# Two FFN batches at a time by seven block products, and gate products on ScalarE, in a fused attention and mixture-of-depths kernel

## The chip, the cores and the metric

One Trainium2 core. Its engines run instruction queues of their own: PE (TensorE, matrix products; PEld is its weight loads), ACT (ScalarE), DVE (VectorE), POOL (GpSimd), and SP, which issues most DMAs. The time is the device time of one execution in microseconds (us). A second number, the span, comes from a profiled execution: from the first to the last instruction that the hardware profiler recorded.

## The reference

For 8 batches of 8 heads, 1152 tokens and head dimension 64, all float32, queries are averaged in pairs, so there are 576 rows per batch. Attention is followed by a mixture of depths: the 128 rows of each batch with the best gate score pass through a two-layer FFN and are added back, weighted.

```
q_pool = q.reshape(B, H, S // 2, 2, D).mean(axis=3)
attn   = softmax(q_pool @ k.T / sqrt(D)) @ v         # (B, H, 576, 64)
x      = attn rearranged to (B, 576, 512)
scores = x @ w_gate
for b in range(B):
    top = the 128 rows with the largest scores[b]
    xe  = x[b, top]
    h   = maximum(xe @ w1, 0)                        # w1: 512 x 1024
    ye  = h @ w2                                     # w2: 1024 x 512
    out[b, top] = xe + sigmoid(scores[b, top]) * ye  # other rows: out = x
```

## The kernel before

The class `_Plain` writes out each engine's order by hand; no scheduler moves anything. A pair is two heads of a batch, and a half is 288 of a pair's 576 query rows: 8 batches x 4 pairs x 2 = 64 halves, numbered h = 0 to 63; s is h mod 2. The loop in `run` issues for half h, in this order:

- at s=1, on SP's queue: `load_pair` (keys `kb`, queries `qb`) and `load_values` (`v_sb`) of the pair two further on, and `stored`, the output rows of an earlier pair;
- `scores(h)`: nine PSUM tiles of products of keys and queries on PE (L818), each turned into `p` by an exp on ACT (L825);
- ACT copies of row sums: `side_by_side` at s=0 (L887, `groups`), `spread` at s=1 (L902, `sums`, which reads `total`, a DVE reduction at L893);
- `units(mid=True)`: pieces of the FFN work of an earlier batch that are marked "mid". These come between the scores and the values product on PE;
- `gated` (DVE: L979 and L981), `folded` (POOL adds tiles of `p` to `acc`, L857; DVE reduces, L862 and L872), and `multiplied`, on POOL (L925): `prod` = `avb` times the gate weights;
- at s=0, `prepare_pair` for the next pair (POOL L732, DVE transposes L735 and L739);
- `weighted(h-1)`: the values product on PE (L836) and its copy `two` on ACT (L844), which frees the PSUM tile; then POOL adds its two parts into `av` (L846) and DVE transposes that into `avb` (L915);
- `added` (L893) at s=0, `normalized` at s=1 (DVE `rec` L954, POOL `x` L956), and `units(mid=False)`, the other pieces.

An engine takes its instructions in the order in which they were issued: a piece put at "mid" stands behind the exps of half h and ahead of `two` of half h-1.

All PE results share one pool of four PSUM tiles of two banks each (`banks`). The FFN of a batch is a generator, `routed(b)`, created when the batch's gate scores are complete (half 8b+10). Its pieces for batches 0 to 5: `groups` of the score line on ACT in half 8b+11; DMA of the line through DRAM; the rank of each row by comparison on DVE (L1083, L1092, L1102) in halves 8b+13 to 8b+15; picks (L1166), `index` (L1175) and the gathering indirect DMA of 128 rows into `xe` (L1183, POOL's queue) in 8b+16; transposes on PE (L1197) in 8b+18; layer 1 (L1208, with relu on ACT, L1216) at mid of 8b+19; layer 2 (L1221) at mid of 8b+20; then scaling on ACT (L1240), addition on POOL (L1245) and a scattering indirect DMA. Batch 5's layer 2 and most of batches 6 and 7 come after the last half, in `run`'s last lines (`older`, `old` and `new` are batches 5, 6 and 7). L1044 is a DVE product, `diag`, of batch 7 only.

Of the kernel before, what the change touches and what calls it, by code (L numbers as in the profile page):

```python
# [10 lines left out]
P = 128  # L11
BLK = 32
# [522 lines left out]
class _Plain:  # L535
# [10 lines left out]
    def __init__(self, ctx, tc, q, k, v, moe_w_gate, moe_w1, moe_w2, capacity, out):  # L546
# [27 lines left out]
        assert 0 < self.TAIL < P and self.Dm == self.ND * P and self.Dm <= 512  # L574
        assert self.F == self.NFC * P and self.NFC % 4 == 0
# [15 lines left out]
        self.w_gate = self.const.tile([P, self.NPAIR, BLK], F32, name="w_gate")  # L591
        self.w1 = self.const.tile([P, self.ND, self.F], F32, name="w1")
        self.w2 = self.const.tile([P, self.NFC, self.Dm], F32, name="w2")

# [21 lines left out]
    def constants(self):  # L616
# [13 lines left out]
        slot_i = self.ffn.tile([P, self.Sp], I32, name="cmp", bufs=1)  # L630
        nc.gpsimd.iota(slot_i[:, :], pattern=[[1, self.Sp]], base=0, channel_multiplier=0)
        self.slot_f = const.tile([P, self.Sp], F32, name="slot_f")
        nc.vector.tensor_copy(self.slot_f[:, :], slot_i[:, :])
# [34 lines left out]
    def line_of_scores(self):  # L668

        line = self.ffn.tile([P, self.NT * P], F32, name="sc_row")  # L670
        self.nc.gpsimd.memset(line[0:1, self.Sp :], 0.0)
        return line
# [11 lines left out]
    def load_gate(self):  # L684
        gate = self.w_gate_in.rearrange("(n j d) -> n j d", n=self.NPAIR, j=2)
        for j, ds, rows in self.quarters():
            self.nc.sync.dma_start(self.w_gate[rows, :, :], _rows_of(gate[:, j, ds], BLK))
# [9 lines left out]

    def load_pair(self, b, hp):  # L700

        nc = self.nc
        kb = self.load.tile([P, self.KB, BLK], F32, name="kb")
        qb = self.load.tile([P, self.QB, 2, BLK], F32, name="qb")
        for j, ds, rows in self.quarters():
            of = self.k[b, 2 * hp + j, :, ds]
            nc.sync.dma_start(kb[rows, :, :], of.rearrange("(i n) d -> i n d", i=BLK))
        for j, ds, rows in self.quarters():
            of = self.q[b, 2 * hp + j, :, ds].rearrange("(i m) d -> i m d", i=BLK)
            nc.sync.dma_start(qb[rows, :, :, :].rearrange("i n r d -> i (n r) d"), of)  # L710
        return {"k": kb, "q": qb, "b": b, "hp": hp}

    def load_values(self, pair):


        nc, hp = self.nc, pair["hp"]
        v_sb = pair["v"] = self.load.tile([P, 2, self.NC, self.D], F32, name="v_sb", bufs=3)
        of = self.v[pair["b"], 2 * hp : 2 * hp + 2]
        of = of.rearrange("j (i g c) d -> g i j c d", i=BLK, c=self.NC)
        for g in range(P // BLK):  # L720
            nc.sync.dma_start(
                v_sb[g * BLK : (g + 1) * BLK, :, :, :].rearrange("i j c d -> i j (c d)"),
                of[g].rearrange("i j c d -> i j (c d)"),
            )
# [16 lines left out]
    def load_first(self, b, hp):  # L741
# [3 lines left out]
        kb = self.load.tile([P, self.KB, BLK], F32, name="kb")  # L745
        kn = kb.rearrange("p n d -> p (n d)").rearrange("p (c j d) -> p c j d", c=NC, j=2)
        acc = self.work.tile([P, G, 2 * self.HALF], F32, name="acc")
        third = self.QB // 3
        qn = acc.rearrange("p u n -> p (u n)")[0 : 3 * BLK, 0 : 4 * third * D]
        qn = qn.rearrange("p (j m d) -> p j m d", j=2, d=D)  # L750
        v_sb = self.load.tile([P, 2, NC, D], F32, name="v_sb", bufs=3)
# [11 lines left out]
        return {"k": kn, "q": qn, "v": v_sb, "b": b, "hp": hp}  # L763

    def prepare_first(self, pair):
# [5 lines left out]
        acc = self.work.tile([P, G, 2 * self.HALF], F32, name="acc")  # L771
        qp = acc.rearrange("p u n -> p (u n)")[0:rows, 0 : 2 * third * D]
        qp = qp.rearrange("p (n j d) -> p n j d", j=2, d=D)
# [76 lines left out]
    def folded(self, half):  # L850
# [9 lines left out]
        fold = self.small.tile([P, 2, G * nb], F32, name="fold")  # L860
# [21 lines left out]
    def side_by_side(self, of):  # L882

        n = of.shape[-1]
        to = self.small.tile([BLK, P // BLK, n], F32, name="groups")
# [33 lines left out]
    def multiplied(self, half):  # L919

        pair, hb, hp = half["pair"], self.HB, half["pair"]["hp"]
        if half["s"] == 0:
            pair["prod"] = self.work.tile([P, self.QB, BLK], F32, name="prod")
        ns = slice(half["s"] * hb, (half["s"] + 1) * hb)
        self.nc.gpsimd.tensor_tensor(  # L925
            out=pair["prod"][:, ns, :],
            in0=pair["avb"][:, ns, :],
            in1=self.w_gate[:, hp : hp + 1, :].broadcast_to([P, hb, BLK]),
            op=ALU.mult,
        )  # L930
# [42 lines left out]
    def gated(self, half):  # L973
# [5 lines left out]
        nc.vector.tensor_reduce(pair["red"][:, ns], pair["prod"][:, ns, :], AX.X, ALU.add)  # L979
# [17 lines left out]
    def routed(self, b, part):  # L997
# [13 lines left out]
        if b < self.B - 1:  # L1011
# [17 lines left out]
            sc_row = ffn.tile([P, NT * P], F32, name="sc_row")  # L1029
# [11 lines left out]
        else:  # L1041

            diag = ffn.tile([P, self.QB, BLK], F32, name="diag", bufs=1)
# [34 lines left out]
        for t, rows in tiles:  # L1078
            at = t * P
            cmp = ffn.tile([P, Sp], F32, name="cmp", bufs=1)  # L1080
# [20 lines left out]
            tie = ffn.tile([P, P], F32, name="tie", bufs=1)  # L1101
# [35 lines left out]
        for s0, w in self.slots:  # L1137
            pick = ffn.tile([P, NT, P], F32, name="pick", bufs=1)
            index = ffn.tile([P, 1], I32, name="index")
            own_gate = ffn.tile([P, 1], F32, name="own_gate")  # L1140
            if b == self.B - 1:
# [3 lines left out]
                    in0=self.slot_f[:, s0 : s0 + w].unsqueeze(1).broadcast_to([P, NT, w]),  # L1145
# [36 lines left out]
            xe = ffn.tile([P, self.Dm], F32, name="xe")  # L1182
# [18 lines left out]
            yield mid  # L1201

            hT = ffn.tile([P, self.NFC, P], F32, name="hT")
            for f0 in range(0, self.NFC, 4):
                pv = self.banks()[:, 0, :].rearrange("p (c n) -> p c n", n=P)
                for f in range(4):
                    for c in range(self.ND):
                        nc.tensor.matmul(  # L1208
                            pv[:, f, 0:w],
                            lhsT=self.w1[:, c, (f0 + f) * P : (f0 + f + 1) * P],  # L1210
                            rhs=xeT[:, c, 0:w],
                            start=(c == 0),
                            stop=(c == self.ND - 1),
                        )
                    if f == 3:
                        nc.scalar.activation(hT[:, f0 : f0 + 4, 0:w], pv[:, :, 0:w], AF.Relu)  # L1216
                    yield "hidden" if f0 + f == self.NFC - 1 else False

            ps = self.banks()[:, 0, :]
            for f in range(self.NFC):  # L1220
                nc.tensor.matmul(  # L1221
                    ps[0:w, 0 : self.Dm],
                    lhsT=hT[:, f, 0:w],
                    rhs=self.w2[:, f, :],
                    start=(f == 0),
                    stop=(f == self.NFC - 1),
                )
                yield False
            if b == self.B - 1:
                nc.vector.scalar_tensor_tensor(  # L1230
                    out=xe[0:w, :],
                    in0=ps[0:w, 0 : self.Dm],
                    scalar=own_gate[0:w, 0:1],
                    in1=xe[0:w, :],
                    op0=ALU.mult,
                    op1=ALU.add,
                )
            else:
                y = ffn.tile([P, self.Dm], F32, name="y", bufs=1)
                nc.scalar.activation(  # L1240
                    y[0:w, :], ps[0:w, 0 : self.Dm], AF.Copy, scale=own_gate[0:w, 0:1]
                )
                if b < self.B - 2:
                    yield True
                nc.gpsimd.tensor_tensor(out=xe[0:w, :], in0=y[0:w, :], in1=xe[0:w, :], op=ALU.add)  # L1245
            nc.gpsimd.indirect_dma_start(
                out=rows_out,
                out_offset=bass.IndirectOffsetOnAxis(ap=index[0:w, 0:1], axis=0),
                in_=xe[0:w, :],
                in_offset=None,  # L1250
                bounds_check=(b + 1) * Sp - 1,
                oob_is_err=False,
            )
            yield True

    def counted(self):
# [3 lines left out]
        flags = self.ffn.tile([P, n], F32, name="cmp", bufs=1)  # L1260
# [46 lines left out]
    def run(self):  # L1307
# [10 lines left out]
        if loaded:  # L1318
            self.load_values(loaded)
        self.load_gate()  # L1320
        weights = self.weight_loads()
        for h in range(n_halves + 1):
            if h < n_halves:
# [6 lines left out]
                else:  # L1330
                    loaded = None
                    if n + 2 < len(pairs):
                        loaded = self.load_pair(*pairs[n + 2])
                        self.load_values(loaded)
                    if n > 1:
                        self.stored(halves[h - 4]["pair"])
                if h > 1:
                    next(weights, None)
                half = {"pair": pair, "s": s}
                halves.append(half)  # L1340
                self.scores(half)
                if h > 1:

                    of = halves[h - 2 - s]["pair"]
# [8 lines left out]
                if h > 1:  # L1353
                    self.multiplied(halves[h - 2])
# [42 lines left out]
        pieces(older, self.NFC - 2)  # L1397
        pieces(new, 1)
        pieces(older, 2)
        pieces(new, 3)  # L1400
        pieces(older)
        pieces(old, self.NFC)
        pieces(new, 1)
        low = self.counted()
        pieces(old, self.NFC - 3)
# [66 lines left out]
```

## The time and the profile before

| | |
|---|---|
| runs | 708.6, 706.26, 708.48 us; median 708.48 |
| profiled execution | 706.64 us; span 704.8 us; granted PE clock 0.998 |
| busy, share of the span | PE 99%, PEld 73%, DVE 70%, ACT 63%, POOL 69% |
| DMA | 82.86 MB, mean 118 GB/s |
| largest groups, busy us | L825 320.2 (ACT), L818 295.2 and L836 294.6 (PE), L857 266.3 (POOL), L862 251.3 (DVE) |
| FFN on PE, busy us | L1208 59.3, L1221 57.3 |

Busy time counts an instruction from its start to its end, so a DVE or POOL instruction that waits inside its span counts as busy. A line such as L1208 is a line of the kernel before. In a group's line the columns are: line, engine, operation, output and inputs with their shapes, count; busy us, mean ns of one; idle time of the engine ahead of them and what ended it.

### The profile page before, as it was taken

To read this page: it belongs to the slowest core of one execution; us is meant where nothing else is said; L and a number is where in the kernel's file an instruction comes from. 1 tells how busy PE (TensorE), PEld (TensorE's weight loads), DVE (VectorE), ACT (ScalarE), POOL (GpSimd) and SP (SyncE) were. 2 spreads that over 40 slices of the span, in tenths; PEclk is the share of its full clock that TensorE was granted. 3 is DMA by queue.
4 is the path that set the end of the run, shared out by engine and by line. 5 is a ranking of instruction groups with operands and counts; after the bars stand their busy time and mean duration, and the time that the engine had idled before them with its cause. 6 is when DMAs were issued, how large, how long until landed. Compare 5 with 4: busy or idle time off the path is not lost.

```text
span 704.8 us, 23397 instructions
## 1 busy us (share of the span) xinstructions
PE 694.4 (99%) x9948; PEld 516.8 (73%) x9948; DVE 496.5 (70%) x793; ACT 444.5 (63%) x963; POOL 485.1 (69%) x452
## 2 busy tenths in 40 slices
PE   8999999999999999999999999999999999999996
PEld 5668899996758866688656887578775787766573
DVE  3877777996559965498754988559774697689540
ACT  6677778777547775477746776467754777477210
POOL 5877777868658695586955779467874877686520
PEclk9999999999999999999999999999999999999999
DMA  8888887858486483756928468382775728432200
GB/s 175 172 178 180 171 166 137 146 116 161 85 149 111 85 162 75 145 97 111 172 40 159 81 129 160 66 148 61 161 130 85 135 56 169 83 72 62 45 31 35
DMA packets 389490, 82.86 MB, mean 118 GB/s; under 512 B 376640, under 2 KB 376640, under 8 KB 389376
## 3 DMA queue, kind: packets, MB, share of 16 engines
q1 hardware_dynamic: 387872, 76.49, 58.1%
q0 software_dynamic: 1280, 4.20, 1.8%
q8 instruction: 80, 1.31, 0.8%
q10 hardware_dynamic: 224, 0.59, 0.3%
q14 instruction: 34, 0.28, 0.1%
HBM read 69.65 MB, written 11.59 MB: 115 GB/s over the span
## 4 chain that ended last, share of the span: by engine, by line
PE 89%; POOL 5%; issue 2%; DMA 1%; ACT 1%; DVE 1%; SPq 0%; POOLq 0%; DVEq 0%; ACTq 0%
PE ps L836 36%; PE ps L818 36%; PE ps L1208 8%; PE ps L1221 7%; POOL acc L857 2%; ACT p L825 1%; DMA kb<-in_k_dram 1%; DMA xe<-out_dram,index 1%; PE ps L1197 1%; POOL prod L925 1%; POOL x L956 0%; POOL av L846 0%; DVE fold L862 0%; POOL index L1175 0%; SPq L759 0%
## 5 line engine op out<-in xcount | busy, mean ns | idle before, releaser
L825 ACT ACTIVATE p<-ps 128x576 f32<-128x576 f32 x576 | 320.2, 695 | 1.7 <-PE ps L818 1.3
L818 PE MATMUL ps<-qT,kT 64*64 64x288 f32 x4608 | 295.2, 404 | 0.2 <-ACT p L825 0.2
L836 PE MATMUL ps<-p,v_sb 64*64 64x288 f32 x4608 | 294.6, 403 | 0.0
L857 POOL TENSOR_TENSOR acc<-p 128x576 f32<-128x576 f32 x192 | 266.3, 1417 | 15.4 <-ACT p L825 15.1
L836 PEld LDWEIGHTS ps<-p,v_sb 64*64 64x64 f32 x4608 | 215.5, 133 | 65.3 <-ACT p L825 9.2
L818 PEld LDWEIGHTS ps<-qT,kT 64*64 64x64 f32 x4608 | 208.0, 132 | 73.0 <-ACT p L825 15.4
L862 DVE TRANSPOSE_TENSOR_REDUCE fold<-p 128x54 f32<-128x1728 f32 x64 | 126.0, 1969 | 50.2 <-ACT p L825 50.2
L862 DVE TRANSPOSE_TENSOR_REDUCE fold<-acc 128x54 f32<-128x1728 f32 x64 | 125.3, 1957 | 46.0 <-POOL acc L857 45.8
L844 ACT COPY two<-ps 128x576 f32<-128x576 f32 x64 | 40.9, 639 | 156.9 <-PE ps L836 143.8
L846 POOL TENSOR_TENSOR av<-two 128x288 f32<-128x288 f32 x64 | 51.2, 800 | 96.5 <-ACT two L844 94.9
L915 DVE STREAM_TRANSPOSE avb<-av 128x288 f32<-128x288 f32 x64 | 29.4, 460 | 66.5 <-POOL av L846 66.5
L956 POOL TENSOR_TENSOR x<-avb,rec 128x576 f32<-128x576 f32 x32 | 37.1, 1159 | 40.3 <-DVE rec L954 27.9
L1208 PEld LDWEIGHTS ps<-xeT,w 128*128 128x128 f32 x512 | 57.8, 192 | 2.7 <-ACT p L825 2.6
L1208 PE MATMUL ps<-xeT,w 128*128 128x128 f32 x512 | 59.3, 277 | 0.0
L1221 PE MATMUL ps<-w,hT 128*128 128x512 f32 x128 | 57.3, 598 | 0.0
L925 POOL TENSOR_TENSOR prod<-avb,w_gate 128x288 f32<-128x288 f32 x64 | 51.5, 805 | 0.6 <-DVE avb L915 0.6
L902 ACT ACTIVATE sums<-total,tiny 32x18 f32<-32x18 f32 x124 | 38.1, 308 | 15.9 <-DVE total L893 14.2
L732 POOL TENSOR_TENSOR qp<-qb 128x576 f32<-128x576 f32 x31 | 43.8, 1414 | 2.2 <-DMA qb<-in_q_dram 2.2
L1221 PEld LDWEIGHTS ps<-w,hT 128*128 128x128 f32 x128 | 23.6, 190 | 28.1 <-issue 25.8
L735 DVE STREAM_TRANSPOSE kT<-kb 128x1152 f32<-128x1152 f32 x31 | 42.5, 1370 | 0.0
L887 ACT COPY groups<-sum 32x36 f32<-32x36 f32 x124 | 27.1, 219 | 6.7 <-DVE sum L872 5.2
L981 DVE TENSOR_TENSOR part<-red,rec 128x18 f32<-128x18 f32 x32 | 27.0, 845 | 1.1
(95 smaller groups left out, 290.6 us busy)
## 6 DMA issues: line engine op xcount, KB each, us to landing
kb<-in_k_dram SPq DMA_DIRECT2D x124, 144.0 KB
qb<-in_q_dram SPq DMA_DIRECT2D x124, 144.0 KB
v_sb<-in_v_dram SPq DMA_DIRECT2D x124, 144.0 KB
out_dram<-x SPq DMA_DIRECT2D x128, 72.0 KB
lines<-row_rank SPq DMA_DIRECT2D x7, 640.0 KB
w<-in_moe_w_dram SPq DMA_DIRECT2D x8, 512.0 KB
sc_row<-row SPq DMA_DIRECT2D x7, 288.0 KB
acc<-in_q_dram ACTq DMA_DIRECT2D x2, 288.0 KB
```

The lines of the kernel that those rows point to most:

```text
L732: nc.gpsimd.tensor_tensor(out=qp[:, :, :], in0=pair["q"][:, :, 0, :], in1=pair["q"][:, :, 1, :], op=ALU.add)
L735: nc.vector.transpose(kT.rearrange("p (c g i) -> p c g i", c=self.NC, i=BLK), pair["k"].rearrange("p (g c) d -> p c g d", c=self.NC),)
L818: nc.tensor.matmul(sc[keys, j, 0:n], lhsT=pair["kT"][rows, c * P + keys.start : c * P + keys.stop], rhs=pair["qT"][rows, qs], start=True, ...
L825: nc.scalar.activation(p[:, c // G, c % G, :, :], sc[:, :, 0:n], AF.Exp, scale=self.scale)
L836: nc.tensor.matmul(av[j * self.D : (j + 1) * self.D, e, 0:n], lhsT=half["pair"]["v"][keys, j, c, :], rhs=half["p"][keys, c // G, c % G, j, :],
L844: nc.scalar.copy(two[:, :, :], av[:, :, 0:n])
L846: nc.gpsimd.tensor_tensor(out=half["av"][:, :], in0=two[:, 0, :], in1=two[:, 1, :], op=ALU.add)
L857: nc.gpsimd.tensor_tensor(out=acc[:, u, :], in0=units[:, 0, u, :], in1=units[:, 1, u, :], op=ALU.add)
L862: nc.vector.tensor_reduce(fold[:, a, :], of.rearrange("p u (m d) -> p (u m) d", d=BLK), AX.X, ALU.add, apply_transpose=True,)
L925: self.nc.gpsimd.tensor_tensor(out=pair["prod"][:, ns, :], in0=pair["avb"][:, ns, :], in1=self.w_gate[:, hp : hp + 1, :].broadcast_to([P, ...
L1208: nc.tensor.matmul(pv[:, f, 0:w], lhsT=self.w1[:, c, (f0 + f) * P : (f0 + f + 1) * P], rhs=xeT[:, c, 0:w], start=(c == 0), stop=(c == self ...
L1221: nc.tensor.matmul(ps[0:w, 0 : self.Dm], lhsT=hT[:, f, 0:w], rhs=self.w2[:, f, :], start=(f == 0), stop=(f == self.NFC - 1),)
```

## The change

Batches 0 to 5 are taken in pairs (0,1), (2,3), (4,5). The 256 rows of a pair and the weights are cut into 2 x 2 blocks, and each layer is computed with seven block products instead of eight (Winograd's form of Strassen's scheme), with sums of blocks before and after:

- Layer 1 of a pair: seven products of eight matmuls of 128 columns, in one "mid" piece of half X = 28, 44, 60. Layer 2: seven products of four matmuls of 256 columns, at mid of half X+4 = 32 and 48, and for the third pair after the last half.
- Sums of weight blocks (`weight_sums`): eight DVE subtractions of 128x1024 in the odd halves 11 to 25, each stored to DRAM; `load_sums` brings the set of one layer (2 MB) back into `tw` before each use.
- Sums of input blocks (`input_sums`): four POOL operations per layer and pair; 128x256 for layer 1 in halves X-2 and X-1, 128x512 for layer 2 in halves X+2 and X+3.
- ACT copies each product from PSUM to SBUF as PE finishes a PSUM tile of two products. Seven DVE additions follow per layer and pair (128x512 for layer 1, 128x256 for layer 2), issued behind the values product of the half, that is, ahead of DVE's work of the next half.
- Relu is now an ACT operation from SBUF to SBUF of 128x1024 for each batch, at mid of halves X+1 and X+2. Scaling by the gate comes at mid of X+5, addition and scatter in X+5 and X+6.
- Gate products: `multiplied` is an ACT operation on `av` (before the transposition, one weight per partition), issued right behind the exps; L925 on POOL is gone. `gated`'s DVE reduction transposes as it reads.
- Space: `kb` and `qb` have one buffer instead of two, `v_sb` two instead of three (`load_values` is issued one pair later), and the scratch of the ranks and picks shares a buffer.
- The order of pieces after the last half is new; the third pair's seven products stand between pieces of batches 6 and 7.

The core of the diff:

```diff
+        self.paired = self.B - 2 - self.B % 2
+        self.tw = self.const.tile([P, 4, self.ND // 2 * self.F // 2], F32, name="tw")
...
+    def weight_sums(self):
...
+            for i, (to, x, y) in enumerate(((t1, b12, b11), (t2, b22, t1), (t3, b22, b12), (t4, b21, t2))):
+                nc.vector.tensor_tensor(out=to, in0=x, in1=y, op=ALU.subtract)
+                nc.sync.dma_start(kept[:, i, :], self.tw[:, i, :])
+                yield
+
+    def load_sums(self, layer):
+        for i in range(0, 4, 2):
+            self.nc.sync.dma_start(self.tw[:, i : i + 2, :], self.tw_kept[layer][:, i : i + 2, :])
+            yield
...
-        kb = self.load.tile([P, self.KB, BLK], F32, name="kb")
-        qb = self.load.tile([P, self.QB, 2, BLK], F32, name="qb")
+        kb = self.load.tile([P, self.KB, BLK], F32, name="kb", bufs=1)
+        qb = self.load.tile([P, self.QB, 2, BLK], F32, name="qb", bufs=1)
...
-        v_sb = pair["v"] = self.load.tile([P, 2, self.NC, self.D], F32, name="v_sb", bufs=3)
+        v_sb = pair["v"] = self.load.tile([P, 2, self.NC, self.D], F32, name="v_sb", bufs=2)
...
     def multiplied(self, half):
-        self.nc.gpsimd.tensor_tensor(
-            out=pair["prod"][:, ns, :],
-            in0=pair["avb"][:, ns, :],
-            in1=self.w_gate[:, hp : hp + 1, :].broadcast_to([P, hb, BLK]),
-            op=ALU.mult,
+        half["prod"] = self.small.tile([P, self.HALF], F32, name="prod", bufs=2)
+        hp = half["pair"]["hp"]
+        self.nc.scalar.activation(
+            half["prod"][:, :], half["av"][:, :], AF.Copy, scale=self.w_gate[:, hp : hp + 1]
         )
...
+    def seven_products(self, layer, a, s, c, rest, shape):
...
+        steps = (
+            (a11, b11, c11, ()),
+            (s1, t1, c22, ()),
+            (s3, t3, c21, ()),
+            (s2, t2, u, ((u, c11), (c21, u), (u, c22), (c22, c21))),
+            (s4, b22, c12, ((c12, u),)),
+            (a12, b21, x, ((c11, x),)),
+            (a22, t4, y, ((c21, y),)),
+        )
+        copies = []
+        for i, (of, by, to, _) in enumerate(steps):
+            if i % 2 == 0:
+                tile = self.banks()
+            ps, n = shape(tile[:, i % 2, :]), of.shape[1]
+            for f in range(by.shape[2] // P if layer == 1 else 1):
+                for k in range(n):
...
+                    nc.tensor.matmul(
+                        args[0], lhsT=args[1], rhs=args[2], start=k == 0, stop=k == n - 1
+                    )
+
+            copies.append((to, ps))
+            last = i == len(steps) - 1
+            if i % 2 or last:
+                for copy in copies:
+                    nc.scalar.copy(*copy)
+                copies = []
+            yield last
+        for *_, sums in steps:
+            for to, of in sums:
+                nc.vector.tensor_tensor(out=to, in0=to, in1=of, op=ALU.add)
+
+    def layers_of_two(self, tokens):
...
+        yield from self.seven_products(1, a, s, c, rest, lines)
+        loads = self.load_sums(2)
+        next(loads)
+        yield "mid"
+        for i, tile in enumerate(hidden):
+            nc.scalar.activation(tile[:, :, 0:w], tile[:, :, 0:w], AF.Relu)
+            yield True if i else "mid"
...
@@ run
                     if n + 2 < len(pairs):
                         loaded = self.load_pair(*pairs[n + 2])
-                        self.load_values(loaded)
+                    if n + 1 < len(pairs):
+                        self.load_values(upcoming)
...
+                if h > 10 and s == 1:
+                    next(sums, None)
...
                 self.scores(half)
                 if h > 1:
+                    self.multiplied(halves[h - 2])
...
                 self.folded(half)
-                if h > 1:
-                    self.multiplied(halves[h - 2])
...
-        pieces(older, self.NFC - 2)
+        pieces(older, 3)
         pieces(new, 1)
-        pieces(older, 2)
+        pieces(older, 1)
         pieces(new, 3)
-        pieces(older)
-        pieces(old, self.NFC)
+        pieces(older, 4)
+        pieces(old, self.NFC // 2 - 1)
+        pieces(older, 1)
         pieces(new, 1)
         low = self.counted()
-        pieces(old, self.NFC - 3)
+        pieces(old, self.NFC // 2 + 1)
+        pieces(older)
         pieces(new, 2)
         pieces(old)
```

## The prediction

> **What bounds the kernel now.** I read the page's busy shares and chain of waits first, to see which engine sets the end:
>
> ```profile
> PE 694.4 (99%) x9948; PEld 516.8 (73%) x9948; DVE 496.5 (70%) x793; ACT 444.5 (63%) x963; POOL 485.1 (69%) x452
> PE 89%; POOL 5%; issue 2%; DMA 1%; ACT 1%; DVE 1%; SPq 0%; POOLq 0%; DVEq 0%; ACTq 0%
> ```
>
> TensorE (PE) has no free time, so less work on it is a gain, and any wait that reaches it is a loss. Then the groups, for what the change touches:
>
> ```profile
> L1208 PE MATMUL ps<-xeT,w 128*128 128x128 f32 x512 | 59.3, 277 | 0.0
> L1221 PE MATMUL ps<-w,hT 128*128 128x512 f32 x128 | 57.3, 598 | 0.0
> L925 POOL TENSOR_TENSOR prod<-avb,w_gate 128x288 f32<-128x288 f32 x64 | 51.5, 805 | 0.6 <-DVE avb L915 0.6
> ```
>
> A float32 matmul shows as two records, so 512 records are the 32 matmuls of eight batches' first layers. Then the timeline of PE and of ACT over batch 0's FFN (start, duration, line; the last number is the count, the bracket the idle time before):
>
> ```profile
> 171.64 4.54 PE L818 MATMUL ps<-qT,kT 64*64 64x288 f32 x72
> 176.12 7.41 PE L1208 MATMUL ps<-xeT,w 128*128 128x128 f32 x64
> 183.46 4.60 PE L836 MATMUL ps<-p,v_sb 64*64 64x288 f32 x72
> 187.88 4.54 PE L818 MATMUL ps<-qT,kT 64*64 64x288 f32 x72
> ...
> 171.95 0.64 ACT L844 COPY two<-ps 128x576 f32<-128x576 f32 x1 [1.49 <-PE ps L836]
> 172.48 5.00 ACT L825 ACTIVATE p<-ps 128x576 f32<-128x576 f32 x9
> 179.91 1.27 ACT L902 ACTIVATE sums<-total,tiny 32x18 f32<-32x18 f32 x4 [2.42 <-DVE total L893]
> 181.21 0.85 ACT L887 COPY groups<-line 32x18 f32<-32x18 f32 x4
> ```
>
> Half 19 is 16.24 us long, a half without FFN 8.73. In it ACT waits 2.42 for `total`, unseen, because L1208 keeps PE busy. In an ordinary odd half ACT has 2.48 us idle before the next `two`, in an even one 1.91: that is the cover of all that the change puts on ACT.
>
> The last view is the timeline of DVE and POOL in one place:
>
> ```profile
> 169.34 0.21 DVE L954 RECIPROCAL rec<-sums 128x18 f32<-128x18 f32 x1
> 169.91 0.92 DVE L981 TENSOR_TENSOR part<-red,rec 128x18 f32<-128x18 f32 x1
> ...
> 169.64 1.16 POOL L956 TENSOR_TENSOR x<-avb,rec 128x576 f32<-128x576 f32 x1 [1.48 <-DMA out_dram<-x]
> ```
>
> Both DVE lines handle 18 columns. The one with two inputs in SBUF takes 0.92 instead of 0.21 and ends 0.03 after POOL's running step: it waited that step out. All 32 of L981 lie at 0.62 to 0.92.
>
> **The sum**, against the profiled execution (706.64 us: span 704.8 and 1.84 around it). The median of the runs is 708.48, another 1.84 above; I add that at the end.
>
> *1. FFN on PE, a gain of 10.5.* A record of 128 columns takes 59.3/512 = 0.1158, one of 512 takes 57.3/128 = 0.4477; a straight line through both gives 0.2264 for 256. Layer 1 of a pair: 128 records, 14.83, become 7 x 8 matmuls = 112 records, 12.97: -1.85. Layer 2: 32 records, 14.33, become 28 matmuls = 56 records of 256, 12.68: -1.65. Three pairs: -10.5. If 256 columns cost half of 512 and each insertion is priced by the longer half (7.5 and 7.2), it is -11.0; if the short passes eat layer 2's saving, -5.6. That 128 columns cost nearly a quarter of 512 speaks for the straight line.
>
> The Trainium skill ("TensorE: Matmul & The Clock Gate", Back-to-back issue gap) gives for a stream of weight load and matmul 81 ns at 128 columns and 131 at 512, which speaks against short passes: by its proportion 256 columns would cost some three quarters of 512, and layer 2 would lose 4.4 a pair. The ratio in this trace is 3.87, not 1.62; the row decides. The page's other figure, for a single matmul (columns/2.4 + 2.5 ns), has the ratio seen here.
>
> *2. The relu behind the added sums, a loss of 8.9 (1.3 to 8.9).* Call X the half with a pair's first layer (28, 44, 60). DVE's seven adds of 128x512, all between SBUF tiles, come after it, ahead of the folds of half X+1. ACT's queue in X+1 holds nine exps, the gate product, the four sums, the relu of the first hidden tile, and only then `two`, which frees the PSUM tile of the values product. An add: L1044 takes 0.76 for 128x576, so 0.68 each, 4.8 together. They stand behind `avb`, which follows `two` (at 0.3, 0.64 long) and `av` (0.80), so undisturbed they run from about 2.0 to 6.8 us into X+1. ACT gets to the relu at 7.2 (L902 at 5.9 and four times 0.32): no wait; the relu (by L844's 0.64 and L1240's 0.69, about 1.0) and gate product (0.4) fit into the 2.48. Only X=60 is late, by 1.3, because two ranks of the next batch (each L1083, L1092 and L1102, about 1.4) stand ahead on DVE. If each add waits out a POOL step as L981 does, and POOL takes its next step between two adds, POOL's 3 x 1.42 (L857), 0.80 (L846) and 1.16 (L956) lie among them: 4.8 + 6.2 = 11.0. The relu ends at 12.0, `two` was due at 8.73 + 0.3: 2.9 late. PE runs ahead of ACT by about 0.2 in the scores, so it stalls 2.7, twice, and 3.5 at X=60: 8.9. I take the upper end, since L981, the nearest row, is of that kind in all 32.
>
> The Trainium skill ("SBUF — State Buffer", Who interferes with whom) states this as a lock held for a whole instruction, in both directions. The trace shows one direction; by the other each L857 among the adds is 0.68 later, which the alternation above already holds.
>
> *3. Halves that lose their cover, a loss of 3.9 (0 to 4.1).* Half 8b+19 had L1208 of batch b. Now batches 0, 1 and 3 have nothing there (X and X+4 are other halves), but ACT's wait for `total` stays: it hangs on L862, that on POOL's third L857, behind gather and index steps. L902 starts about 8.3 into the half, its four take 1.27, the groups of `line` 0.85 and their issue: `two` at 10.5 instead of 9.0. Less the 0.2: 1.3 each. Zero if POOL, rid of L925, gets to L857 sooner; but L956 and L735 stand in the way too, so I keep it.
>
> *4. Rank chain and tail, a loss of 2.5 (0.5 to 4).* Eight subtracts of 128x1024 on DVE (1.35 by L1044) at halves 11 to 25; four sit near a rank chain. Gathers landed 0.64 and 0.67 us ahead of L1197 for batches 0 and 1 (166.00 for 166.64, 251.55 for 252.22): 1.2 later makes 0.55 of stall each. In the tail ACT's two scales of the third pair wait for DVE's adds, ahead of batch 7's index copies: 0.8 to 1.2; batch 6's gather 0.5.
>
> *5. Input sums of layer 2, a loss of 1.6 (0 to 5).* POOL's four 128x512 sums (1.28 each by L857) wait for the relus and must be ready for the third product at halves 32 and 48: 0.8 each. The third pair's lie in the tail, counted above.
>
> *6. At nothing:* POOL's 51.5 of L925 are off the path (POOL 69%). ACT's gate products, 64 x 0.4, lie in the 1.9 to 2.5. ACT's copies of products (0.3 to 0.6) follow PE tile by tile inside an insertion of 13 us. Loads: `v_sb` now comes one half later and `kb`, `qb` have one buffer; 14.7 MB more goes to and from DRAM. DMA carries 118 GB/s in the mean and 180 at its best, and the values have by my count of SP's queue some 5 us to spare. If not, PE waits up to 5 at each reload of 2 MB: +10.
>
> Sum: -10.5 + 8.9 + 3.9 + 2.5 + 1.6 = +6.4, so 713.0 by the profile's measure, 714.9 as a median.
>
> **The rivals.**
>
> *Faster: the adds find POOL idle.* Without L925 POOL is busy about 6.3 of 8.73 us (3 x 1.42, 0.80 and half of 1.16 and 1.41); if the adds of X+1 fall ahead of the first exps' L857, or if a wide add does not wait as an 18-column one does, step 2 shrinks to 1.3, step 3 to 1, 4 to 1 and 5 to 0: -10.5 + 3.3 = -7.2, so 701.3. It decides whether DVE's last add ends before 8.2 us into X+1. For it: POOL's 0.8 us less a half. Against it: the accs of half X itself are still running when the adds start, and all 32 of L981 waited.
>
> *No change: the adds run free, but steps 3 to 5 stand:* -10.5 + 1.3 + 3.9 + 2.5 + 1.6 = -1.2: 707.3.
>
> *Slower still:* loads late (+10 beside the forecast, part of it hiding step 2: 720), or no saving in layer 2 (-5.6 instead of -10.5: 719.8). The slices show DMA at most 180 GB/s; PE idles 0.2 us in all of L818 before, so no load was late then.
>
> *The change does not do what it says:* if the seven products are not shorter on PE, only losses are left, 725; the records of two widths speak against it.
>
> **How the numbers follow.** Forecast 714.9: 0.38; faster rival 701.3: 0.31; in between 707.3: 0.19; slower still, about 720: 0.12. What a measurement of this kernel can tell from no change is 0.5%, 3.5 us: 704.9 to 712.0. So faster 0.31, same 0.19, slower 0.50. The range goes from 700 (the faster rival, less 1 for the bound of step 1) to 721 (the late loads); outside lie a faster case with every step free, 698, and the broken one: 2 in 10. The forecast's own range is 711 to 718.
>
> **What would show it.** Right: the matmuls of the products take 39 us (3 x 12.97) and 38 (3 x 12.68); in halves 29, 45 and 61 ACT's relu waits for DVE's adds, an add's mean is above 1.3 us, and PE has gaps of 2 to 3.5 us at the scores after; `two` waits on `line`'s groups in halves 19, 27 and 43. Wrong: adds of 0.7 us; relus that start as soon as ACT reaches them; PE still gapless at those halves. The forecast falls if PE's idle time stays below 10 us, and step 6 if PE waits for `v_sb` or for the summed weights.

## The result and the profile after

The changed kernel takes 760.77 us (median of 4 runs, 760.37 to 763.41) against 707.88 for the kernel before, run beside it: a ratio of 1.0759, 95% interval 1.0727 to 1.079. It is 53 us slower. The prediction said slower by 6.4, with a range that ended at 721. The direction was right; the size was wrong by a factor of eight.

In the changed kernel's lines, L845 and L863 are the products of scores and values, L871 `two`, L884 POOL's `acc`, L734 and L748 the loads of keys and of values, L717 and L722 the stores and loads of the weight sums, L1159 and L1163 the DMAs of the ranks, L1194 the picks, L1214 the gather, L1228 the transposes of the gathered rows, L1351 the seven products, L1359 their copies, L1364 the additions, L1390 relu, L1410 scale, L1317 the input sums.

The page's busy shares and the row of PE's granted clock:

```profile
PE 704.1 (93%) x9972; PEld 547.9 (72%) x9972; DVE 550.1 (72%) x842; ACT 490.9 (65%) x1063; POOL 465.9 (61%) x411
PEclk9999999998999899999999999999999899999999
```

PE was 99% busy before and is 93% now, and its busy time rose by 10 although it has less to do; its mean granted clock is 0.968 instead of 0.998. The waits of PE (how long in all, how often, longest) say at what it stood:

```profile
PE ps L1228 <- DMA xe<-out_dram,index: 12.2, 3, 5.7
PE ps L845 <- ACT two L871: 11.7, 6, 2.9
PE ps L863 <- DMA v_sb<-in_v_dram: 10.3, 2, 5.4
PE ps L1351 <- POOL s L1317: 3.9, 2, 1.9
PE ps L1082 <- DVE rank_parts L1104: 3.0, 1, 3.0
```

The first and third are waits for loads that the prediction priced at little or nothing; the second is the stall that it had foreseen, in more places. Here is half 18 on PE's timeline, with the transposes of batch 0's gathered rows, first before and then after:

```profile
161.96 4.75 PE L818 MATMUL ps<-qT,kT 64*64 64x288 f32 x72
166.64 0.66 PE L1197 MATMUL ps<-ident,xe 128*128 128x128 f32 x4
167.23 4.60 PE L836 MATMUL ps<-p,v_sb 64*64 64x288 f32 x72
```
```profile
162.42 4.64 PE L845 MATMUL ps<-qT,kT 64*64 64x288 f32 x72
172.74 1.09 PE L1228 MATMUL ps<-ident,xe 128*128 128x128 f32 x4 [5.68 <-DMA xe<-out_dram,index]
173.76 6.83 PE L863 MATMUL ps<-p,v_sb 64*64 64x288 f32 x72
180.41 4.54 PE L845 MATMUL ps<-qT,kT 64*64 64x288 f32 x72
184.78 4.59 PE L863 MATMUL ps<-p,v_sb 64*64 64x288 f32 x72
```

A wait of 5.68, and behind it the same 72 records take 6.83 us instead of 4.59. The windows (us, busy times, then the granted clock, DMA share, GB/s) give the clock: 0.66 just behind the wait, 1.00 at the next product of values.

```profile
173.70:180.50 6.80, 6.80 (x77) 3.75 (x80) 5.81 (x8) 1.89 (x6) 4.55 (x5) 0.66 0.79 168
184.80:189.30 4.50, 4.50 (x80) 3.75 (x80) 4.50 (x7) 3.94 (x12) 4.06 (x3) 1.00 0.47 75
```

So behind this wait PE loses another 2.7 us: 0.43 at the transposes and 2.24 at the next product. The half lasts 17.99 us (start of one L845 group to the next) instead of 9.68; batch 1's 17.24 instead of 9.74; the two halves with late values 15.95 and 16.13 instead of 8.73. Together these four halves take 30.4 us more.

SP's queue shows a good part of where the gather lost its time. Its longest waits before and after, then the stretch of batch 0's ranks before and after:

```profile
SPq L1131 <- DVE red L979: 71.6, 7, 17.1
```
```profile
SPq L734 <- DVE kT L762: 120.1, 19, 20.8
```
```profile
142.36 3.52 SPq L968 DMA_DIRECT2D out_dram<-x  x4
150.31 0.36 SPq L1131 DMA_DIRECT2D row_rank<-both  x1
153.06 0.36 SPq L1135 DMA_DIRECT2D lines<-row_rank  x1
```
```profile
151.17 3.67 SPq L990 DMA_DIRECT2D out_dram<-x  x4
154.94 0.57 SPq L717 DMA_DIRECT2D tw<-tw  x1
155.60 0.38 SPq L1159 DMA_DIRECT2D row_rank<-both  x1
159.21 0.32 SPq L1163 DMA_DIRECT2D lines<-row_rank  x1
```

Before, SP stood waiting for the ranks and sent them as soon as DVE had them (150.31 for batch 0). After, DVE has `both` ready at 151.9, 1.6 later than before, and SP comes to it only at 155.60, 3.7 later still: the loads of keys ahead of it on the queue had waited for the one `kb` to be transposed (issued from 139.94, before from 131.38), and a store of weight sums stands between. `lines` is issued at 159.21 instead of 153.06, and the pick on DVE starts at 165.0 instead of 159.0.

The seven products themselves came as predicted. Three insertions of layer 1 take 12.78 us each (12.97 said); a run of 16 records of the third pair's layer 2, undisturbed in the tail, 3.62, or 0.226 per record of 256 columns (0.2264 said).

### The profile page after: what moved, and what is told of

The parts are those of the page before. It is cut to its first block, busy times and chain, and to the rows that moved or that the text cites. A ratio compares the mean times of both kernels' runs of the same rounds, so it can differ in the third digit from the quotient of the medians.

```text
span 758.9 us, 23703 instructions
## 1 busy us (share of the span) xinstructions
PE 704.1 (93%) x9972; PEld 547.9 (72%) x9972; DVE 550.1 (72%) x842; ACT 490.9 (65%) x1063; POOL 465.9 (61%) x411
## 5 line engine op out<-in xcount | busy, mean ns | idle before, releaser
L863 PE MATMUL ps<-p,v_sb 64*64 64x288 f32 x4608 | 304.5, 411 | 10.4 <-DMA v_sb<-in_v_dram 10.3
L845 PE MATMUL ps<-qT,kT 64*64 64x288 f32 x4608 | 303.1, 409 | 11.7 <-ACT two L871 11.7
L884 POOL TENSOR_TENSOR acc<-p 128x576 f32<-128x576 f32 x192 | 272.7, 1449 | 16.5 <-ACT p L852 16.2
L863 PEld LDWEIGHTS ps<-p,v_sb 64*64 64x64 f32 x4608 | 225.9, 135 | 73.8 <-issue 18.3
L845 PEld LDWEIGHTS ps<-qT,kT 64*64 64x64 f32 x4608 | 218.0, 134 | 81.7 <-ACT two L871 15.0
L871 ACT COPY two<-ps 128x576 f32<-128x576 f32 x64 | 40.8, 638 | 107.0 <-PE ps L863 106.6
L950 ACT ACTIVATE prod<-av,w_gate 128x288 f32<-128x288 f32 x64 | 36.1, 564 | 31.4 <-POOL av L873 30.6
L929 ACT ACTIVATE sums<-total,tiny 32x18 f32<-32x18 f32 x124 | 37.9, 306 | 10.3 <-DVE total L920 9.1
L766 DVE STREAM_TRANSPOSE qT<-qp 128x576 f32<-128x576 f32 x31 | 23.0, 742 | 11.3 <-POOL qp L759 11.3
L1001 DVE TRANSPOSE_TENSOR_REDUCE red<-prod 128x9 f32<-128x288 f32 x64 | 29.1, 455 | 0.0
L1120 DVE TENSOR_SCALAR_CACHE_REDUCE pick<-sc_row,gate_sc 128x576 f32<-128x576 f32 (+4 forms) x40 | 21.6, 539 | 5.4 <-ACT gate_sc L682 5.2
L1203 POOL TENSOR_SCALAR index<-found_token 128x1 int32<-128x1 f32 x7 | 6.4, 918 | 30.8 <-DVE pick L1194 30.8
```

Of the source, the lines that this page charges most:

```text
L845: nc.tensor.matmul(sc[keys, j, 0:n], lhsT=pair["kT"][rows, c * P + keys.start : c * P + keys.stop], rhs=pair["qT"][rows, qs], start=True, ...
L863: nc.tensor.matmul(av[j * self.D : (j + 1) * self.D, e, 0:n], lhsT=half["pair"]["v"][keys, j, c, :], rhs=half["p"][keys, c // G, c % G, j, :],
L871: nc.scalar.copy(two[:, :, :], av[:, :, 0:n])
L884: nc.gpsimd.tensor_tensor(out=acc[:, u, :], in0=units[:, 0, u, :], in1=units[:, 1, u, :], op=ALU.add)
L929: self.nc.scalar.activation(tot[rows, :], pair["total"][:, j * self.QB : (j + 1) * self.QB], AF.Identity, bias=self.tiny[0:BLK, 0:1],)
L950: self.nc.scalar.activation(half["prod"][:, :], half["av"][:, :], AF.Copy, scale=self.w_gate[:, hp : hp + 1])
```

## Experiments

**1. The buffers alone, the gate products alone, the traffic, the buffers back.**

```diff
 first: kernel before
-        kb = self.load.tile([P, self.KB, BLK], F32, name="kb")      # and qb
+        kb = self.load.tile([P, self.KB, BLK], F32, name="kb", bufs=1)
-        ... name="v_sb", bufs=3)
+        ... name="v_sb", bufs=2)            # and load_values(upcoming), one pair later
 second: kernel before
+        multiplied(), gated(), load_gate() of the changed kernel
 third: changed kernel
-                nc.sync.dma_start(kept[:, i, :], self.tw[:, i, :])
-            self.nc.sync.dma_start(self.tw[:, i : i + 2, :], self.tw_kept[layer][:, i : i + 2, :])
 fourth: changed kernel
-        self.tw = self.const.tile([P, 4, ...
+        self.tw = self.const.tile([P, 2, ...            # sums i and i+2 share a place
-        ... name="kb", bufs=1)                           # and qb
+        ... name="kb")
+        ... name="total", bufs=3)     # to make room; red and line 2, instead of 4
```

Expected of the first: 

> The kernel before with one buffer for kb and qb, two for v_sb and the values loaded one pair later; nothing else. Theory Q (queue: with one buffer a load of keys waits for the transposes of the pair before it, and everything behind it on SP's queue, the rank DMAs among it, waits too): PE waits 4 to 6 us at the transposes L1197 of batches 0 to 5, 5 to 8 us more per batch with the lower clock after it, 735 to 755 us. Theory T (traffic: the stores and loads of the weight sums are what makes the gathers late): 706 to 712 us, gathers land where they did. The prediction's step 6 (loads at nothing) also says no more than 712.

Expected of the second: 

> The kernel before with the gate products on ScalarE and the transposing reduction on DVE; nothing else. The prediction's step 6 (hidden in ACT's 1.9 to 2.5 us ahead of two): 705 to 710 us, ACT's gap before two smaller by 0.4. Rival (the product waits for POOL's av and holds ACT back): 712 to 720 us, with ACT waiting for av ahead of the sums.

Expected of the third: 

> The changed kernel without the stores of the weight sums to DRAM and without the loads that bring them back (the products then use whatever sums lie in the tile, so half of them are of the other layer). Theory T: the gathers of batches 0 and 1 and both late values are in time, 725 to 732 us. Theory Q: the late values (about 15 us with the lower clock) go, because 2 MB no longer lie ahead of them, but the transposes of batches 0 and 1 still wait about 3 to 5 us each: 738 to 748 us.

Expected of the fourth: 

> The changed kernel with two buffers for kb and qb again; to make room, the tile of weight sums holds two sums instead of four, so the first two are overwritten by the last two, while stores and loads keep their number and size. Theory Q: the transposes of batches 0 and 1 wait under 1 us and the late values mostly go: 728 to 738 us. Theory T: as the changed kernel, 755 to 762 us.

Measured (us; in brackets the ratio to the kernel before run beside it, and its 95% interval): first 707.57 (0.9998, 0.9977 to 1.0019); second 712.81 (1.0075, 1.0047 to 1.0104); third 735.06 (1.0382, 1.034 to 1.0424); fourth 737.4 (1.0415, 1.0372 to 1.0458). In the third and fourth, and in two runs of group 3, the products use sums that are not theirs or are not added up; these runs serve for the time alone.

Neither theory held as written. The buffers alone cost nothing (against theory Q), and yet giving the buffers back with all the traffic kept takes 23.4 us away (against theory T); taking the traffic away takes 25.7. PE's waits for gathers and values in the fourth:

```profile
PE ps L1228 <- DMA xe<-out_dram,index: 5.7, 4, 2.5
PE ps L863 <- DMA v_sb<-in_v_dram: 0.7, 1, 0.7
```

The first run shows why the buffers alone do no harm. SP is late in it, too (`row_rank` at 154.80, before at 150.31), but the gather goes out at 162.87 instead of 161.19: the pick used to wait its turn on DVE until 159.0, and that slack takes most of it.

```profile
SPq L707 <- DVE kT L735: 142.9, 29, 13.0
```
```profile
PE ps L1197 <- DMA xe<-out_dram,index: 2.5, 3, 1.6
```

So the buffers spend the slack. What the traffic adds for batch 0 can be read from the third run, which has the single buffers without it, against the changed kernel:

```profile
154.13 0.77 SPq L1157 DMA_DIRECT2D row_rank<-both  x1
156.79 0.36 SPq L1161 DMA_DIRECT2D lines<-row_rank  x1
161.02 0.88 DVE L1192 SCALAR_TENSOR_TENSOR pick<-lines,token,token_line 128x640 f32<-128x640 f32 x1 [0.92 <-DMA lines<-row_rank]
```
```profile
164.98 0.88 DVE L1194 SCALAR_TENSOR_TENSOR pick<-lines,token,token_line 128x640 f32<-128x640 f32 x1 [4.32 <-DMA lines<-row_rank]
```

With the traffic `row_rank` goes out 1.5 us later, and then the two transfers are slower: 3.61 us from `row_rank` to `lines` instead of 2.66, and 5.77 from `lines` to the pick instead of 4.23. Of the 4.0 us that the pick is later, the place on the queue is the smaller part and the slower transfers are the larger.

The gate products, which the prediction had at nothing, cost 5.3 us (3.3 to 7.4): the time of the rival, but not by its path. It is not ACT's gap before `two` (no PE wait for `two` is shown); PE waits for six gathers:

```profile
PE ps L1196 <- DMA xe<-out_dram,index: 7.0, 6, 1.8
```

Batch 1's gather is issued at 246.79 (before: 246.71) and lands at 253.84 (before: 251.55). It is not this transfer alone. The profile's row of the main DMA queue (packets, MB, share of 16 engines' span that their packets took), before and with the gate products on ScalarE:

```profile
q1 hardware_dynamic: 387872, 76.49, 58.1%
```
```profile
q1 hardware_dynamic: 387824, 76.42, 63.1%
```

By the spans (704.8 and 709.1) nearly the same bytes took 409 us before and 447 here. The other kernels without stored sums divide in the same way: 432 to 444 with the gate products on ScalarE, 400 to 404 with them on POOL. Why the transfers are slower beside them, no run shows.

**2. Relu and scale later, the sums on another queue, the additions on POOL, and a first smaller version.**

```diff
 first: changed kernel, layers_of_two, ahead of the relus and ahead of the scales
+        yield True
 second
-                nc.sync.dma_start(kept...          # and the load
+                nc.gpsimd.dma_start(kept...
 third, seven_products
-                nc.vector.tensor_tensor(out=to, in0=to, in1=of, op=ALU.add)
+                nc.gpsimd.tensor_tensor(out=to, in0=to, in1=of, op=ALU.add)
 fourth: layers_of_two with seven products for layer 1 only; layer 2 as L1221, batch by batch
-        for layer in (2, 1):                       # weight_sums, no store, no load
+        for layer in (1,):
         # gate products on POOL; total, line and y with 3, 2 and 1 buffers
```

Expected of the first: 

> The changed kernel with the two relus of layer 1 and the two scales of layer 2 each issued one half later (relus at mid of X+2 and X+3, layer 2 at X+5, scales at X+7), so that DVE's added sums are done when ACT reaches them. Theory R (ACT waits for DVE's adds ahead of two, and PE's scores wait for two): about 8.5 us at the relus and 9 us at the scales go, 740 to 748 us. Rival (the lateness stays on DVE and POOL and only shows elsewhere, at the input sums or the gathers): 752 to 762 us.

Expected of the second: 

> The changed kernel with the stores and loads of the weight sums issued on POOL's DMA queue instead of SP's; the same bytes. Theory Q (what stands behind them on SP's queue waits): the waits for gathers of batches 0 and 1 and for the values shrink from 21 us to under 8, 730 to 740 us. Rival B (the bytes themselves fill the DMA engines, whichever queue issues them): the waits stay above 15 us, 750 to 765 us.

Expected of the third: 

> The changed kernel with the 42 additions behind the products on POOL instead of DVE (128x512 about 1.28 us, 128x256 about 0.73 by POOL's input sums). Theory L (DVE's adds are long because they wait for POOL's steps in turn): no two-input add waits any more; at X+1 POOL takes 7 x 1.28 = 9.0 before the accs, so the relu starts at about the same time as now and the exps' accs are late instead: 755 to 768 us. Rival (POOL has the room): scores no longer wait for two, 743 to 750 us.

Expected of the fourth: 

> A version that keeps of the change what the runs so far support: only layer 1 goes in pairs by seven products; its four weight sums are made once (halves 11 to 17), stay in the tile, and are never stored or loaded; gate products are back on POOL; the relus come one half later; layer 2 is as in the kernel before, at mid of X+4 and X+5. Buffers as in the changed kernel. Theory: layer 1 gains 5.6 to 6.1 us, single buffers alone cost nothing (707.6 measured), 1 to 3 us lost at gathers and in the tail: 701 to 706 us. Rival (halves 8b+19 without cover, step 3 of the prediction, cost 3.9, and the longer insertions collide): 706 to 713 us.

Measured: first 772.58 (1.0913, 1.0867 to 1.0959); second 763.36 (1.0783, 1.0744 to 1.0822); third 762.23 (1.0767, 1.0726 to 1.0807); fourth 723.45 (1.0221, 1.0192 to 1.025).

The first was a miss, outside both ranges: the waits moved on, as its rival said, and grew. In it PE waited 11.5 us for POOL's input sums (3.9 in the changed kernel) and 22.6 for gathers. In the second the waits for the gathers of batches 0 and 1 (4.4) and for values (7.5) did shrink, to 11.9, less than theory Q said, but those for `two` rose to 18.2, and the time is in rival B's range. It does not separate the queue from the bytes, because on POOL's queue a store holds up POOL: at 150.82 one goes out that had waited for DVE's subtraction (done at 150.53), and POOL's `acc`, whose exps had ended at 143.49, starts behind it at 151.44. In the third, POOL did the additions in no better time for the whole, as theory L said. The fourth, with no traffic at all, is still 2.2% slower than the kernel before, outside both of its ranges. PE waits in it 7.1 us for `two` and 9.6 for gathers.

**3. Both cures, no additions, no pairs, and layer 1 away from the ranks.**

```diff
 first: the third and fourth edit of group 1 together
 second: changed kernel without stores and loads of the weight sums, and
-                nc.vector.tensor_tensor(out=to, in0=to, in1=of, op=ALU.add)
 third: changed kernel (tail order as before)
-        self.paired = self.B - 2 - self.B % 2
+        self.paired = 0
 fourth: the smaller version of group 2, with
+        self.paired = self.B - 4
+        for _ in range(6):                         # five halves later: X = 33, 49
+            yield True
```

Expected of the first: 

> The changed kernel with both cures at once: no stores and loads of the weight sums (735.1 alone) and two buffers for kb and qb (737.4 alone, with the tile of sums cut to two); the products use whatever sums are in the tile. Theory I (the loss of some 25 us needs both, the single buffers and the traffic, so either cure takes all of it): 731 to 736 us, no more gained. Rival (two losses of their own, of 25 and 23): 710 to 716 us.

Expected of the second: 

> The changed kernel without the traffic of the weight sums (735.1) and also without the 42 DVE additions behind the products, so the products are not summed. Theory L (the additions, long because they wait for POOL, hold up ACT's relus and scales, and these hold up two and the scores; and they make DVE late for POOL's input sums): the scores' waits for two fall from 13.5 us to under 3, and the layer-2 insertions from 16.2 to under 14: 714 to 722 us. Rival (ACT's and DVE's lateness comes from ranks and gate products, the additions only stand in it): 728 to 735 us.

Expected of the third: 

> The changed kernel with no batch in a pair: single buffers, gate products on ScalarE, the shared scratch, but the FFN and the tail as in the kernel before. If the parts add up (707.6 for the buffers alone, 712.8 for the gate products alone, against 707.1): 711 to 715 us. If they work on each other, 717 to 725 us. Either way the pairs cost the rest to 760.8.

Expected of the fourth: 

> Layer 1 in pairs only for batches 0 to 3 (gain 2 x 1.95 = 3.9 us), placed five halves later than in the changed kernel (X = 33 and 49), where DVE has no ranks of a later batch to do; weight sums made in halves 6 to 9, kept, no traffic; gate products on POOL; relus at X+2 and X+3, layer 2 as before at X+4 and X+5; batch 4's layers six halves later. Theory C (in the version before it, 723.5, DVE's additions met the ranks of the next batch in halves X+1 to X+3, and total, sum and so two were late): no score waits for two above 0.5 us, 702 to 708 us. Rival (the relus and the lost cover cost it anyway): 711 to 718 us.

Measured: first 736.19 (1.0419, 1.039 to 1.0447); second 714.55 (1.0112, 1.0083 to 1.0142); third 722.33 (two runs, 718.97 and 725.69; 1.0223, 1.0161 to 1.0284); fourth 732.87 (1.0376, 1.0352 to 1.04).

The first settles theory I: both cures together give no more than either. The 25 us need the single buffers and the traffic at once.

The second is the largest single answer: without the 42 additions, 20.5 us less. ACT's waits for them, then PE's for `two`, without the traffic and with the additions:

```profile
ACT y L1408 <- DVE y L1362: 12.8, 3, 5.1
ACT hT L1388 <- DVE hT L1362: 8.8, 3, 3.9
```
```profile
PE ps L843 <- ACT two L869: 13.5, 7, 2.9
```

and PE's without them:

```profile
PE ps L843 <- ACT two L869: 1.8, 2, 1.6
```

The layer-2 insertion at X+4, 16.2 us in the changed kernel, falls to 12.35.

The third shows that the buffers and the gate products together, without any pair, cost some 16 us, not the 5 to 6 that their parts add up to; PE waits 10.7 us for gathers in it. The two runs lie 7 us apart, so only 11 to 20 is said. This kernel also has the shared scratch of the ranks and picks, which no run tests alone; a part of the 16 may be its.

In the fourth theory C fell, and the rival's range with it. The input sums were late (6.0 us of PE's waits), and `two` still waited for ACT. It shows the prediction's step 3 plainly: in halves 19 and 27, which had lost their layer 1, ACT stood for `total` until past the end of the half, and the next half took 1.9 and 2.1 us longer than 8.73. No version here beats the kernel before, and none that was tried comes within 1% of it with pairs.

The runs form a ladder from one kernel to the other: 706.4 before; 722.3 with single buffers, gate products and shared scratch; 714.6 with the products in pairs, without additions and without stored sums; 735.1 with the additions; 760.8 with the stores and loads.

## Why the prediction was right or wrong

**Step 1, the gain on PE, held.** 12.78 and, undisturbed, 0.226 per record against 12.97 and 0.2264. The straight line between 128 and 512 columns was right, and the figures that the Trainium skill ("TensorE: Matmul & The Clock Gate", Back-to-back issue gap) gives for a stream, 81 and 131 ns, were not those of this trace (0.116 us at 128 columns, 0.448 at 512). The range's -5.6 did not come.

**Step 2, mechanism right, its size right by luck, one place left out.** The additions do wait for POOL, and some longer than one of its steps. DVE in the half after batch 0's and 1's layer 1, and after their layer 2, then POOL at the same two places:

```profile
292.28 0.66 DVE L1364 TENSOR_TENSOR s<-s,hT 128x512 f32<-128x512 f32 x1
293.70 1.78 DVE L1364 TENSOR_TENSOR s<-s,hT 128x512 f32<-128x512 f32 x1
295.52 1.78 DVE L1364 TENSOR_TENSOR hT<-hT 128x512 f32<-128x512 f32 x1
...
347.59 0.45 DVE L1364 TENSOR_TENSOR y<-y,s 128x256 f32<-128x256 f32 x1
348.07 5.07 DVE L1364 TENSOR_TENSOR s<-s,y 128x256 f32<-128x256 f32 x1
353.17 0.42 DVE L1364 TENSOR_TENSOR y<-y 128x256 f32<-128x256 f32 x1
```
```profile
293.01 5.56 POOL L884 TENSOR_TENSOR acc<-p 128x576 f32<-128x576 f32 x3 [1.45 <-ACT p L852]
...
347.58 1.11 POOL L1214 DMA_INDIRECT xe<-out_dram,index  x1 [0.28 <-POOL index L1203]
348.71 4.13 POOL L884 TENSOR_TENSOR acc<-p 128x576 f32<-128x576 f32 x3
```

The first addition, with POOL idle, takes 0.66; those beside an `acc` 1.78; one takes 5.07 instead of 0.42, until three `acc` in a row are done (5.08 at the same place of the next pair). The one before it took 0.45 beside the gather's issue, so the issue alone does not hold an addition up. POOL waits too: its three `acc` beside the additions take 5.56 instead of 4.2. In X+1 three of seven waited in each of the first two pairs (1.78, 1.78, 1.89), not all, and one in the third; the stall at the relus was 1.9, 1.9 and about 4.8 (halves of 10.59, 10.59 and a scores run stretched to 9.37), 8.5 in all for the 8.9 said. That the two agree is luck. The prediction let the additions take 11.0 us and then put the relu's end at 12.0, as if they began with the half; by its own 2.0 for their start it is 14.0, and the stall 4.7, 4.7 and 5.5. Against that, the three that waited lost some 3.4 us, where it had 6.2 for all seven. And the sum stopped at the relus. The same pattern stands at the scales: ACT's L1410 sits ahead of `two` and waits for the additions of layer 2, and the prediction had put only the third pair's into its sum (step 4). On PE:

```profile
351.61 1.68 PE L845 MATMUL ps<-qT,kT 64*64 64x288 f32 x24
356.21 4.61 PE L845 MATMUL ps<-qT,kT 64*64 64x288 f32 x48 [2.91 <-ACT two L871]
360.75 0.66 PE L1228 MATMUL ps<-ident,xe 128*128 128x128 f32 x4
```

These halves take 14.1 and 14.4 us where the same halves with a transpose took 9.8 before. The additions' measured price, 20.5 us, holds the relus, the scales, the input sums and part of the tail; steps 2 and 5 together had 10.5.

**Step 3 showed at one of three places in the changed kernel.** Halves 19 and 27 last 8.73 there and no score waits behind them; behind half 43 PE waits 0.69 for `two` instead of the 1.3 said. That the late gathers just ahead of 19 and 27 had given DVE and POOL time is an argument, but other runs bear it out: without the traffic, where batch 1's gather is 1.95 late and not 5.37, PE waits 1.22 behind half 27 and 1.28 behind 43, and the fourth version of group 3, whose gathers were in time, shows halves longer by 1.9 and 2.1.

**Step 4 named the gathers and mis-sized them.** It gave batches 0 and 1 0.55 us each for DVE's subtraction, which was to make the ranks 1.2 later. For batch 0 DVE was 1.6 later; SP's queue added 3.7, and slower transfers the rest. The waits were 5.68 and 5.37, with a lower clock behind each.

**Step 5** had 1.6; PE's waits for L1317 are 3.9, and the layer-2 insertions are 3.5 longer than the 12.68 of step 1, twice.

**Step 6 is the step that failed.** It put the single buffers and 14.7 MB of traffic at nothing, with +10 as the bad end; they cost 25.7 together, and PE waits 10.3 us for `v_sb`, the sign that the prediction had named. The error was to check them one by one. The values had 5 us to spare by SP's count, and single buffers do leave a kernel at 707.6; but the rank DMAs stand on the same queue behind the loads, and the text did not follow them; nor did it count that the transfers themselves become slower with 14.7 MB more, which is the larger part of what they add for batch 0. Nor did it count what a wait of five microseconds does to PE afterwards: 2.2 us more in the next product.

It also had the gate products at nothing. Alone they cost 5.3, and with single buffers and the shared scratch some 16; that this goes through the gathers is seen in PE's waits, and that all transfers are slower beside them in the DMA rows; why is open.

## What to carry to other kernels

When a change takes a buffer away and adds transfers, price both on the queue at once: write out what stands behind each load on the in-order queue, and follow the small DMAs there (here the ranks, on the way to a gather) to the engine that is full, with slower transfers than now. An operation that waits on another engine and stands ahead of the instruction that frees PSUM costs the bound engine whatever of its lateness is left after the slack (here 2.9 us of PE's time for 3.85 of ACT's); list every such place, not the first one found. Where PE is 99% busy, an eighth off 12% of its work is worth 11 us, and four waits of five microseconds, with the lower clock behind them, took 30.

## What the runs showed of the hardware

PE ran at a granted clock of 0.66 for 6.8 us after waiting 5.68 us. After a wait of 1.65 in the smaller version of group 2, the transposes took 0.63 as ever; after waits of 2.95 and 4.35 there, 0.86 and 1.09. The transposes alone do not tell: after a wait of 2.25 in the run without the traffic they took 0.63, but the product behind them 6.29 instead of 4.59.

A two-input addition on DVE waited not for one POOL step but for a run of them: 5.07 and 5.08 us for 128x256 elements in two pairs, the first to 0.3 us after the third `acc` ended. The Trainium skill ("SBUF — State Buffer", Who interferes with whom) says that whoever issues first holds the shared ports for the whole instruction. In this trace the one who waited was passed over by all three `acc`.
